# More zero matmuls in the opening, `v` of block 1 in quarters, and other engines for a few scalings and squares, in a fused attention and MLP kernel

## The chip, the core and the metric

The kernel runs on one core of a Trainium2 chip. Five engines work side by side, each with an instruction stream of its own: TensorE (PE in the profile, with its weight loads as PEld), VectorE (DVE), ScalarE (ACT), GpSimd (POOL) and SyncE (SP). Transfers between the chip's memory and the core's on-chip memory are issued from the queues of SP, ACT and POOL. The metric is the device time of one execution in microseconds (us), lower is better. An execution consists of the span of the core's instructions and about 1.8 us around it.

## The reference

Two stages: a linear attention with a decay per head, in blocks along the sequence, and an MLP with a snake-like activation on its output.

```python
q, k, v: (4, 8, 768, 64) float32     lam: (8,)      # batch, heads, sequence, head size
w_in: (512, 2048)   w_out: (2048, 512)   alpha: (2048,)

# attention, block after block; Dmask holds lam ** (i - j) for j <= i
intra = (qb @ kb.T) * Dmask
out   = intra @ vb + (qb * lam ** (pos + 1)) @ kv_state
kv_state = lam ** block * kv_state + (kb * rev_pow).T @ vb

# MLP on x = out as (3072 tokens, 512)
h = x @ w_in
s = sin(alpha * h)
g = h + s * s / (alpha + 1e-9)
return (g @ w_out).astype(float32)
```

## The kernel before, in words

**Units of work.** The attention is done in 24 steps: step `s` covers one pair of batches, one block of 128 tokens (the kernel takes blocks twice as long as the reference's) and one half of the heads. Two neighbouring steps share a block `d = s // 2` of `k`, `q` and `v`. The MLP is done in 6 chunks of 512 tokens; a chunk needs the attention output of four steps. For chunk `c`, phase A(c) computes `h` for 16 column groups `m` of 128, and phase B(c) multiplies the activations with `w_out` for four token tiles.

**One attention step.** `sec(t=...)` transposes `q` and `k` on TensorE (L482) into a PSUM bank, which is copied out as `qkT` (L667). `sec(s=...)` makes the scores (L494), which VectorE masks into `S_m` (L612). `sec(o=...)` multiplies the masked scores with the scaled `v` (L506), adds the state's part (L516) and forms the state's increment (L529). `put_x` (L625) multiplies the result with a decay table and writes `xT`, the MLP's input; `Zs` (L635, L648) and `Zacc` (L630, L646) keep the state. `prep_v(s)` (L461) scales `v` of a step with `Lv` and rounds it to bf16, on GpSimd or VectorE. For steps 0 to 7 the transposes are TensorE's; from step 8 they are DMA transposes issued from SP (L328).

**One MLP group.** `grp_A(c, m)` does four matmuls into a PSUM bank (L684), ScalarE's sine into `t` (L688), a square into `u` (L695 on ScalarE, L696 on VectorE or GpSimd) and VectorE's `gT = u * r + h` (L698), which reads the bank once more and frees it. `grp_B` accumulates an output tile (L721), ScalarE copies it to `osb` (L728), and SP stores it (L734).

**The opening.** Before the first chunk, the kernel builds masks and decay tables and runs steps 0 to 3. In this stretch TensorE has little to do, and `keep_pe(b, n)` (L422) puts `n` matmuls of 128x128 by 128x512 on zeros into bank `b` between the steps, as ordinary instructions in TensorE's order. `alpha_ops` transposes `alpha` on TensorE and copies it with ScalarE; `alpha_ops2` makes `r = 1 / (alpha + 1e-9)` (aeps on GpSimd, reciprocal on VectorE). The loads of this stretch are issued from POOL's queue: `k`, `q`, `v` of blocks 0 and 1 (L314) and `w_in` in four blocks of four column groups (`w1_block`, L446), then `w_out` in four blocks (L451) and blocks 2 and 3 of `k`, `q`, `v`. With `by_step=True` a `load` is split by step as well as by batch, so that each `prep_v` waits only for its own half of the heads.

**What sets the order.** `rec` hands every operation to a planner with a duration, what it reads and writes, and extra predecessors (`after`). The planner gives it a start time; TensorE and SP take operations in the order of recording, VectorE, ScalarE and GpSimd may take one into an earlier gap of the plan. The program of each engine is then the operations in the order of their planned starts, with semaphore waits where the data asks for them. The order is fixed by the plan; on the chip each engine runs its stream strictly in that order and stands still where a wait is not yet met. Where several engines may do an operation, `fastest` takes the one with the earliest planned end:

```python
def fastest(choices, reads, writes, after=()):
    ...
    return min(choices, key=end)
```

For chunk 1 the square's engine was fixed by `("ACT", "POOL", "DVE")[m % 3]`; for chunks 0, 2 and 3 `fastest` chooses among the three; for chunks 4 and 5 it is given by a table. Inside chunk 0 and 1 phases, `AHEAD_A1` says after which group of A(1) the scalings of steps 8 and 9 are recorded, and `LAST_B0` where the last pieces of B(0) stand between the groups of A(1). From step 8 on, `steady(i)` records the work of step `i` and, two or three steps ahead, the scaling of `v` through `ahead`.

Of the kernel before, what the change touches and what calls it, by code (L numbers as in the profile page):

```python
# [187 lines left out]
def bass_lightning_attn__then__act_snake_kernel(  # L188
# [33 lines left out]
    with es:  # L222
# [20 lines left out]
        Zacc = ring("Zacc", 2, [128, 2, 2 * D], F32)  # L243
# [87 lines left out]
        def clear_pads():  # L331
            for x in q2p:
                rec("DVE", lambda e, x=x: e.memset(x[:, 0:2 * H + 2:2 * H + 1, :], 0.0), 0.1, writes=["pad"])
# [83 lines left out]
        def keep_pe(b, n):  # L417
            z = maskf[:, :].bitcast(BF16)

            def pe(e):  # L420
                for _ in range(n):
                    last = e.matmul(PS[:, b, :], z[:, 0:128], z[:, :])  # L422
                return last
            rec("PE", pe, (0.427 if P.free["PE"] < 5 else 0.216) * n, reads=["maskf"], writes=bk(b))
# [7 lines left out]
                reads=["alpha_r", "identf"], writes=bk(b))  # L432
            rec("ACT", lambda e: e.copy(alpha_sb[:, :], PS[:, b, 0:NM]), 0.2, reads=bk(b), writes=["alpha"])

        def alpha_ops2():
            rec("POOL", lambda e: e.tensor_scalar_add(aeps_sb[:, :], alpha_sb[:, :], 1e-9), 0.2,
                reads=["alpha"], writes=["aeps"])
            rec("DVE", lambda e: e.reciprocal(r_sb[:, :], aeps_sb[:, :]), 0.2, reads=["aeps"], writes=["r"])

        def w_load(fn, keys, slot, n, after):  # L440
            return rec("POOL", fn, 0, writes=keys, slot=slot, nbytes=131072 * n, after=after)
# [29 lines left out]
        def sec(t=None, o=None, s=None, tb=None, sb_=S_BK, ob=O_BK, peek=False, t_engs=("DVE", "ACT"), via=False, x_first=False, z_late=None, later=False):  # L471
# [140 lines left out]
                    rec("DVE", lambda e: e.tensor_tensor(s_out, s_in, mask_b, ALU.mult), 1.25,  # L612
                        reads=keys_s + ["mask.0", "mask.1"], writes=[f"S_m.{s % RS}"])

            def put_O(part=None):
                z = PS[:, ob:ob + 2, 256:384]
                acc = Zacc[ho]
                zs = Zs[o % 3][:, :, :, :].rearrange("p u a d -> p u (a d)")

                def put_x():  # L620
                    x, col = (o // 4) % NX, 256 * (no % 2)
                    xo = xT[x][:, 2 * ho:2 * ho + 2, col:col + 256].rearrange("p a (u i) -> p u a i", u=2)
                    xi = PS[:, ob:ob + 2, 0:256].rearrange("p u (a i) -> p u a i", a=2)
                    X_b = bass.AP(Xt, (2 * ho * NB + no) * 128, [[HS * NB * 128, 128], [0, 2], [NB * 128, 2], [1, 128]])
                    rec("DVE", lambda e: e.tensor_tensor(xo, xi, X_b, ALU.mult), 0.72,  # L625
                        reads=keys_o + [f"X.{2 * ho + a}.{no}" for a in range(2)],
                        writes=[f"x.{x}.{o % 4}"])

                def first_state():
                    rec("ACT", lambda e: e.copy(acc[:, :, :], z), 0.4, reads=keys_o, writes=[f"Zacc.{ho}"])  # L630

                if part != 1 and no > 0:
                    put_x()
                if has_Z and no == 0:
                    rec("ACT", lambda e: e.copy(zs, z), 0.37, reads=keys_o, writes=[f"Zs.{o % 3}"])  # L635
                if no == 0:
                    put_x()
                if part == 0:
                    return
                if has_Z and no == 0:  # L640
                    if z_late is None:
                        first_state()
                    else:
                        z_late.append(first_state)
                elif has_Z:
                    rec("DVE", lambda e: e.tensor_tensor(acc[:, :, :], z, acc[:, :, :], ALU.add), 0.42,  # L646
                        reads=keys_o + [f"Zacc.{ho}"], writes=[f"Zacc.{ho}"])
                    rec("POOL", lambda e: e.tensor_copy(zs, acc[:, :, :]), 0.42,  # L648
                        reads=[f"Zacc.{ho}"], writes=[f"Zs.{o % 3}"])

# [108 lines left out]
        load(0, "k")  # L759
        load(0, "q")  # L760
        consts()
        keep_pe(0, 15)
        iotas()
        consts3()
        load(1, "k")
# [7 lines left out]
        mask_u([P.ops[-1]])  # L773
        sec(t=1, tb=(2, 3), t_engs=("ACT",))
        clear_pads()
        load(0, "v", eng="POOL", by_step=True)
        load(1, "v", eng="POOL")
        w1_block(0, 4)
        w1_block(4, 4)
        decay_table(2, NB, (2, 3))  # L780
        sec(s=0, sb_=4)
        sec(s=1, sb_=6)
        keep_pe(0, 4)
        sec(t=2, tb=(0, 1), t_engs=("ACT",))
        t2 = P.ops[-1]
        sec(t=3, tb=(2, 3), t_engs=("DVE",))
        prep_v(0, ("DVE",))
        sin_table([t2])
        prep_v(1, ("POOL",))
        zl = []  # L790
        keep_pe(4, 2)
        sec(s=2, sb_=0)
        sec(s=3, sb_=2)
        alpha_ops(6)
        prep_v(2, ("POOL",))
        prep_v(3, ("DVE",))
        alpha_ops2()
        w1_block(8, 4)
        w1_block(12, 4)
        sec(o=0, ob=4, z_late=zl)  # L800
        keep_pe(6, 2)
        sec(o=1, ob=6, z_late=zl)
        keep_pe(0, 5)
        o2 = sec(o=2, ob=0, later=True)
        o3 = sec(o=3, ob=2, later=True)
        for f in o2, o3:
            f(0)
        for f in zl:
            f()
        for f in o2, o3:  # L810
            f(1)

        npr = [10]

        def ahead(s):
            while npr[0] <= min(s, NSTEP - 1):
                prep_v(npr[0])
                npr[0] += 1

        def steady(i):  # L820
# [35 lines left out]
                else:  # L856
                    load(d, x, after=[op], us=(u,))

        AHEAD_A1 = {9: 8, 11: 9}
        LAST_B0 = {1: (2, 3), 3: (3, 3)}  # L860
        every, low = range(8), range(4)
        B0_SEC = {3: dict(t=4, tb=(6, 7)), 4: dict(t=5, s=4, tb=(6, 6)), 6: dict(t=6, s=5, tb=(7, 7)),
# [5 lines left out]
        for c in range(NCH):  # L868
            for m in range(NM):
                op = grp_A(c, m, every if m < 12 else (6, 7, 2, 3) if c == 1 else range(2, 4) if m == 15 and c else range(4, 8),  # L870
                      (SQ.get(m, "POOL"),) if c > 3 else (("ACT", "POOL", "DVE")[m % 3],) if c == 1 else ("POOL", "ACT", "DVE"))
                if c == 0:
                    loads(*ISSUE_A0.get(m, ()))
                feed("A", c, m, op)
                if c == 1 and m in AHEAD_A1:
                    prep_v(AHEAD_A1[m], ("POOL",))
                if c == 1 and m in LAST_B0:
                    grp_B(0, *LAST_B0[m], low)
                if c > 1 and m in (3, 7, 11):
                    grp_B(c - 1, 3, m // 4 + 1, low)  # L880
            b_seq = [(s4, m4) for m4 in range(4) for s4 in range(2)] + [(2, m4) for m4 in range(4)] + [(3, 0)]
            if c == 0:
                b_seq = [(s4, m4) for m4 in range(3) for s4 in range(4)] + [(0, 3), (1, 3)]
            if c == NCH - 1:
                b_seq.pop()
            for i, (s4, m4) in enumerate(b_seq):
                if c == 0:
                    loads(*ISSUE_B0.get(i, ()))
                op = grp_B(c, s4, m4, low)
                feed("B", c, i, op)  # L890
                if c == 0 and i in (6, 7, 8, 9):
                    prep_v(i - 2, ("DVE",) if i == 9 else ("POOL",))
                if c == 0 and i in B0_SEC:
                    sec(**B0_SEC[i])
                if c == 1 and i == 0:
                    sec(s=8)
                at = SEC1 if c == 1 else SEC
                if c > 0 and i in at and 4 * (c + 1) + at[i] < NSTEP:
                    steady(4 * (c + 1) + at[i])
# [35 lines left out]
```

## Time and profile before

| What | Value |
|---|---|
| time, median of 13 runs | 224.74 us (223.29 to 227.07) |
| profiled execution: time | 223.29 us |
| profiled execution: span of the core | 221.5 us |
| instructions | 5397 |
| TensorE busy | 201.9 us (91%) |
| VectorE busy | 148.3 us (67%) |
| ScalarE busy | 112.0 us (51%) |
| GpSimd busy | 100.0 us (45%) |
| mean granted TensorE clock | 0.992 |
| moved by DMA | 29.99 MB, mean 135 GB/s |
| `prep_v` on GpSimd / on VectorE | 16 / 8 instructions |

The profiled execution is the fastest of the 13: its time of 223.29 us is 1.79 us more than its span, and 1.45 us below the median. Times inside the profile count from the first instruction. The engines' busy times overlap, so their sum is no time; what counts at each place is which wait ends last there. A line of the timeline gives the start, the duration, the engine and line, what is written from what is read, the shapes, the count, and in square brackets how long the engine had been idle before it and what ended that idle time. Where a wait was for several semaphores, the one that came last is named.

### The profile page before, as it was taken

To read this page: it belongs to the slowest core of one execution; us is meant where nothing else is said; L and a number is where in the kernel's file an instruction comes from. 1 tells how busy PE (TensorE), PEld (TensorE's weight loads), DVE (VectorE), ACT (ScalarE), POOL (GpSimd) and SP (SyncE) were. 2 spreads that over 40 slices of the span, in tenths; PEclk is the share of its full clock that TensorE was granted. 3 is DMA by queue.
4 is the path that set the end of the run, shared out by engine and by line. 5 is a ranking of instruction groups with operands and counts; after the bars stand their busy time and mean duration, and the time that the engine had idled before them with its cause. 6 is when DMAs were issued, how large, how long until landed. Compare 5 with 4: busy or idle time off the path is not lost.

```text
span 221.5 us, 5397 instructions
## 1 busy us (share of the span) xinstructions
PE 201.9 (91%) x2282; PEld 100.4 (45%) x2317; DVE 148.3 (67%) x218; ACT 112.0 (51%) x185; POOL 100.0 (45%) x137
## 2 busy tenths in 40 slices
PE   7458899978999869999999999999999999999994
PEld 3234343444544335444455444455444544444453
DVE  2766699438358986679987688775678764477300
ACT  3952599220389702188923488602568321778030
POOL 7969890313653835247060431235564410555300
PEclk9996999999999999999999999999999999999999
DMA  6999999972899998999999998598900104102044
GB/s 63 145 212 184 202 190 218 206 115 24 97 198 220 243 200 142 224 224 193 220 161 216 175 128 180 109 112 201 155 23 22 29 0 108 37 0 50 0 95 95
DMA packets 69256, 29.99 MB, mean 135 GB/s; under 512 B 53216, under 2 KB 65776, under 8 KB 69232
## 3 DMA queue, kind: packets, MB, share of 16 engines
q0 software_dynamic: 30240, 12.59, 46.6%
q1 hardware_dynamic: 38736, 16.98, 37.3%
q8 instruction: 18, 0.29, 0.6%
q10 hardware_dynamic: 256, 0.08, 0.2%
q14 instruction: 6, 0.05, 0.1%
HBM read 27.28 MB, written 6.29 MB: 152 GB/s over the span
## 4 chain that ended last, share of the span: by engine, by line
PE 76%; DVE 8%; POOL 6%; DMA 4%; issue 3%; ACT 1%; POOLq 0%
PE PS L721 33%; PE PS L684 32%; DMA w<-in_moe_w_in_dram 4%; DVE gT L698 4%; PE PS L506 3%; PE PS L494 2%; PE PS L516 2%; POOL v L314 2%; DVE u L696 2%; DVE S_m L612 2%; PE PS L748 2%; POOL k L314 1%; PE PS L482 1%; POOL q L314 1%; PE PS L529 1%
## 5 line engine op out<-in xcount | busy, mean ns | idle before, releaser
L684 PE MATMUL PS<-xT,w 128*128 128x512 bf16 x376 | 85.7, 379 | 2.4 <-DMA w<-in_moe_w_in_dram 1.0
L721 PE MATMUL PS<-w,gT 128*128 128x512 bf16 x344 | 82.3, 379 | 3.4 <-issue 3.2
L698 DVE SCALAR_TENSOR_TENSOR gT<-u,r_sb,PS 128x512 bf16<-128x512 bf16 x96 | 69.4, 745 | 19.0 <-POOL u L696 13.2
L688 ACT ACTIVATE t<-PS,alpha_sb 128x512 bf16<-128x512 f32 x96 | 63.1, 680 | 23.0 <-PE PS L684 22.1
L684 PEld LDWEIGHTS PS<-xT,w 128*128 128x128 bf16 x384 | 36.8, 98 | 48.1 <-DVE gT L698 2.2
L721 PEld LDWEIGHTS PS<-w,gT 128*128 128x128 bf16 x368 | 34.0, 98 | 39.8
L728 ACT COPY osb<-PS 128x512 f32<-128x512 f32 x23 | 13.4, 584 | 57.1 <-PE PS L721 57.1
L612 DVE TENSOR_TENSOR S_m<-PS,mask 128x1024 bf16<-128x1024 f32 x24 | 29.2, 1222 | 17.2 <-PE PS L494 17.1
L696 POOL TENSOR_TENSOR u<-t 128x512 bf16<-128x512 bf16 x27 | 27.7, 1041 | 26.0 <-ACT t L688 25.8
L461 POOL TENSOR_TENSOR v<-v,Lv 128x512 bf16<-128x512 f32 x16 | 17.3, 1093 | 24.9 <-DMA v<-in_v_dram 24.9
L314 POOL DMA_DIRECT2D k<-in_k_dram x24 | 17.0, 714 | 22.5 <-PE PS L721 17.7
L625 DVE TENSOR_TENSOR xT<-PS,Xt 128x512 bf16<-128x512 f32 x24 | 16.3, 682 | 10.7 <-PE PS L516 10.6
L695 ACT ACTIVATE u<-t 128x512 bf16<-128x512 bf16 x36 | 22.7, 629 | 1.5
L696 DVE TENSOR_TENSOR u<-t 128x512 bf16<-128x512 bf16 x33 | 20.0, 605 | 2.6 <-ACT t L688 2.6
L314 POOL DMA_DIRECT2D q<-in_q_dram x24 | 16.5, 694 | 6.4 <-PE PS L721 4.0
L648 POOL CAST Zs<-Zacc 128x256 bf16<-128x256 f32 x16 | 7.1, 450 | 26.6 <-DVE Zacc L646 26.5
L506 PE MATMUL PS<-S_m,v 64*64 64x128 bf16 x384 | 10.2, 225 | 3.9 <-DVE S_m L612 1.8
L506 PEld LDWEIGHTS PS<-S_m,v 64*64 64x64 bf16 x384 | 6.4, 108 | 13.9 <-issue 9.1
L422 PE MATMUL PS<-maskf 128*128 128x512 bf16 x25 | 8.7, 497 | 1.6 <-DVE maskf L363 1.2
L667 ACT COPY qkT<-PS 128x1024 bf16<-128x1024 bf16 x5 | 5.1, 1012 | 10.1 <-PE PS L482 10.1
L461 DVE TENSOR_TENSOR v<-v,Lv 128x512 bf16<-128x512 f32 x8 | 6.7, 842 | 2.8 <-DMA v<-in_v_dram 2.8
L516 PE MATMUL PS<-qM,Zs 64*64 64x128 bf16 x112 | 8.1, 222 | 0.1
(53 smaller groups left out, 106.4 us busy)
## 6 DMA issues: line engine op xcount, KB each, us to landing
out_dram<-osb SPq DMA_DIRECT2D x46, 128.0 KB, 2.7
v<-in_v_dram SPq DMA_DIRECT2D x16, 256.0 KB, 5.2
k<-in_k_dram POOLq DMA_DIRECT2D x24, 128.0 KB, 4.8
q<-in_q_dram POOLq DMA_DIRECT2D x24, 128.0 KB, 5.0
w<-in_moe_w_in_dram POOLq DMA_DIRECT2D x4, 512.0 KB, 7.9
w<-in_moe_w_out_dram POOLq DMA_DIRECT2D x4, 512.0 KB, 12.7
v<-in_v_dram POOLq DMA_DIRECT2D x6, 256.0 KB, 11.8
v<-in_v_dram POOLq DMA_DIRECT2D x4, 128.0 KB, 4.3
```

The lines of the kernel that those rows point to most:

```text
L314: lambda e, u=u, a=a, h0=h0, h1=h1: e.dma_start(dst[r][half(u), h0:h1, :], a), 0,
L461: rec(eng, lambda e: e.tensor_tensor(v2[c][:, :, :], src, L_b, ALU.mult), dur, reads=reads, writes=writes)
L506: return e.matmul(dst, v2[o % RC][half(u), hid(h, tj), :], S_part(o, u, h, tj), start=start, stop=True, skip_group_check=True)
L612: rec("DVE", lambda e: e.tensor_tensor(s_out, s_in, mask_b, ALU.mult), 1.25, reads=keys_s + ["mask.0", "mask.1"], writes=[f"S_m.{s % RS}"])
L625: rec("DVE", lambda e: e.tensor_tensor(xo, xi, X_b, ALU.mult), 0.72, reads=keys_o + [f"X.{2 * ho + a}.{no}" for a in range(2)], writes=[f" ...
L684: last = e.matmul(PS[:, i, :], w1[:, kc, 128 * m:128 * (m + 1)], xT[x][:, kc, :], start=(kc == 0), stop=(kc == NKC - 1))
L688: rec("ACT", lambda e: e.activation(t16[tt][:, :], PS[:, i, :], ACTF.Sin, scale=alpha_sb[:, m:m + 1]), 0.7, reads=bk(i) + ["alpha"], write ...
L695: return e.activation(u16[tt][:, :], t16[tt][:, :], ACTF.Square)
L696: return e.tensor_tensor(u16[tt][:, :], t16[tt][:, :], t16[tt][:, :], ALU.mult)
L698: rec("DVE", lambda e: e.scalar_tensor_tensor(out=gT[g][:, m, :], in0=u16[tt][:, :], scalar=r_sb[:, m:m + 1], in1=PS[:, i, :], op0=ALU.mul ...
L721: last = e.matmul(PS[:, bank, :], gT[g][:, m, 128 * s4:128 * (s4 + 1)], w2[:, m, :], start=(m == 0), stop=(m == NM - 1))
L728: rec("ACT", lambda e: e.copy(osb[o][:, :], PS[:, bank, :]), 0.6, reads=bk(bank), writes=[f"o.{o}"])
```

## The change

The diff does the following:

- `keep_pe` gets one matmul more at the start (16 instead of 15), a new one after step 1's transposes, and 5, 4, 6, 4 and 2 instead of 4, 2, none, 2 and 5 between the steps that follow: 38 instead of 28.
- Block 1 of `v` is loaded in four quarters, as block 0 was already.
- The second block of `w_in` is recorded after the sine's table load and made to wait for it.
- `v` of step 0 is scaled on GpSimd instead of VectorE. From step 10 on every scaling is given to GpSimd; before, the planner chose.
- Step 0's output part is recorded before `prep_v(3)`. `alpha`'s transpose moves behind step 1, into bank 4, and the reciprocal and the first two `Zacc` additions are tied behind step 3's `put_x`.
- In A(1) the square's engine is the planner's choice instead of a fixed rotation, and for the last two groups it is ScalarE. The scalings of steps 8 and 9 are recorded after groups 13 and 15 instead of 9 and 11.

```diff
--- before.py
+++ after.py
@@ -432,10 +432,10 @@
                 reads=["alpha_r", "identf"], writes=bk(b))
             rec("ACT", lambda e: e.copy(alpha_sb[:, :], PS[:, b, 0:NM]), 0.2, reads=bk(b), writes=["alpha"])
 
-        def alpha_ops2():
+        def alpha_ops2(after):
             rec("POOL", lambda e: e.tensor_scalar_add(aeps_sb[:, :], alpha_sb[:, :], 1e-9), 0.2,
                 reads=["alpha"], writes=["aeps"])
-            rec("DVE", lambda e: e.reciprocal(r_sb[:, :], aeps_sb[:, :]), 0.2, reads=["aeps"], writes=["r"])
+            rec("DVE", lambda e: e.reciprocal(r_sb[:, :], aeps_sb[:, :]), 0.2, reads=["aeps"], writes=["r"], after=after)
 
         def w_load(fn, keys, slot, n, after):
             return rec("POOL", fn, 0, writes=keys, slot=slot, nbytes=131072 * n, after=after)
@@ -612,7 +612,7 @@
                     rec("DVE", lambda e: e.tensor_tensor(s_out, s_in, mask_b, ALU.mult), 1.25,
                         reads=keys_s + ["mask.0", "mask.1"], writes=[f"S_m.{s % RS}"])
 
-            def put_O(part=None):
+            def put_O(part=None, after=()):
                 z = PS[:, ob:ob + 2, 256:384]
                 acc = Zacc[ho]
                 zs = Zs[o % 3][:, :, :, :].rearrange("p u a d -> p u (a d)")
@@ -644,7 +644,7 @@
                         z_late.append(first_state)
                 elif has_Z:
                     rec("DVE", lambda e: e.tensor_tensor(acc[:, :, :], z, acc[:, :, :], ALU.add), 0.42,
-                        reads=keys_o + [f"Zacc.{ho}"], writes=[f"Zacc.{ho}"])
+                        reads=keys_o + [f"Zacc.{ho}"], writes=[f"Zacc.{ho}"], after=after)
                     rec("POOL", lambda e: e.tensor_copy(zs, acc[:, :, :]), 0.42,
                         reads=[f"Zacc.{ho}"], writes=[f"Zs.{o % 3}"])
 
@@ -759,7 +759,7 @@
         load(0, "k")
         load(0, "q")
         consts()
-        keep_pe(0, 15)
+        keep_pe(0, 16)
         iotas()
         consts3()
         load(1, "k")
@@ -773,48 +773,51 @@
         mask_u([P.ops[-1]])
         sec(t=1, tb=(2, 3), t_engs=("ACT",))
         clear_pads()
+        keep_pe(4, 1)
         load(0, "v", eng="POOL", by_step=True)
-        load(1, "v", eng="POOL")
+        load(1, "v", eng="POOL", by_step=True)
         w1_block(0, 4)
-        w1_block(4, 4)
         decay_table(2, NB, (2, 3))
         sec(s=0, sb_=4)
         sec(s=1, sb_=6)
-        keep_pe(0, 4)
+        keep_pe(0, 5)
         sec(t=2, tb=(0, 1), t_engs=("ACT",))
         t2 = P.ops[-1]
         sec(t=3, tb=(2, 3), t_engs=("DVE",))
-        prep_v(0, ("DVE",))
+        prep_v(0, ("POOL",))
         sin_table([t2])
+        w1_block(4, 4, after=[P.ops[-1]])
         prep_v(1, ("POOL",))
         zl = []
-        keep_pe(4, 2)
+        keep_pe(4, 4)
         sec(s=2, sb_=0)
         sec(s=3, sb_=2)
-        alpha_ops(6)
         prep_v(2, ("POOL",))
+        keep_pe(6, 6)
+        sec(o=0, ob=4, z_late=zl)
         prep_v(3, ("DVE",))
-        alpha_ops2()
         w1_block(8, 4)
         w1_block(12, 4)
-        sec(o=0, ob=4, z_late=zl)
-        keep_pe(6, 2)
+        keep_pe(6, 4)
         sec(o=1, ob=6, z_late=zl)
-        keep_pe(0, 5)
+        alpha_ops(4)
+        keep_pe(0, 2)
         o2 = sec(o=2, ob=0, later=True)
         o3 = sec(o=3, ob=2, later=True)
         for f in o2, o3:
             f(0)
+        x3 = [op for op in P.ops if op.eng == "DVE"][-1:]
         for f in zl:
             f()
         for f in o2, o3:
-            f(1)
+            f(1, x3)
+        alpha_ops2(x3)
 
         npr = [10]
 
         def ahead(s):
             while npr[0] <= min(s, NSTEP - 1):
-                prep_v(npr[0])
+                prep_v(npr[0], ("POOL",))
                 npr[0] += 1
 
         def steady(i):
@@ -856,7 +859,7 @@
                 else:
                     load(d, x, after=[op], us=(u,))
 
-        AHEAD_A1 = {9: 8, 11: 9}
+        AHEAD_A1 = {13: 8, 15: 9}
         LAST_B0 = {1: (2, 3), 3: (3, 3)}
         every, low = range(8), range(4)
         B0_SEC = {3: dict(t=4, tb=(6, 7)), 4: dict(t=5, s=4, tb=(6, 6)), 6: dict(t=6, s=5, tb=(7, 7)),
@@ -868,7 +871,7 @@
         for c in range(NCH):
             for m in range(NM):
                 op = grp_A(c, m, every if m < 12 else (6, 7, 2, 3) if c == 1 else range(2, 4) if m == 15 and c else range(4, 8),
-                      (SQ.get(m, "POOL"),) if c > 3 else (("ACT", "POOL", "DVE")[m % 3],) if c == 1 else ("POOL", "ACT", "DVE"))
+                      (SQ.get(m, "POOL"),) if c > 3 else ("ACT",) if c == 1 and m > 13 else ("POOL", "ACT", "DVE"))
                 if c == 0:
                     loads(*ISSUE_A0.get(m, ()))
                 feed("A", c, m, op)
```

## The prediction

> **What bounds the kernel now.** I read the busy rows by slice first, then the chain that ended last, then the timelines around the two stretches in which TensorE stands still.
>
> ```profile
> PE   7458899978999869999999999999999999999994
> PEclk9996999999999999999999999999999999999999
> PE 76%; DVE 8%; POOL 6%; DMA 4%; issue 3%; ACT 1%; POOLq 0%
> ```
>
> A slice is 5.54 us, counted here from 0. From slice 17 (94 us) on TensorE is full, so nothing in the change can gain there. It is thin in slices 0 to 3, in slice 8 (a gap of 0.78 us at 47.7 for which the profile shows no wait, and which the change does not touch) and in slices 13 and 14 (72 to 83 us), the end of A(1). Only in slice 3 is the granted clock low.
>
> The opening ends when the first MLP group starts:
>
> ```profile
> 14.83 0.69 DVE L461 TENSOR_TENSOR v<-v,Lv 128x512 bf16<-128x512 f32 x1 [1.28 <-DMA v<-in_v_dram]
> 15.44 2.35 DVE L612 TENSOR_TENSOR S_m<-PS,mask 128x1024 bf16<-128x1024 f32 x2
> 18.53 1.30 POOL L461 TENSOR_TENSOR v<-v,Lv 128x512 bf16<-128x512 f32 x1
> 21.51 1.52 DVE L625 TENSOR_TENSOR xT<-PS,Xt 128x512 bf16<-128x512 f32 x2 [1.28 <-PE PS L516]
> 23.10 10.06 PEld L684 LDWEIGHTS PS<-xT,w 128*128 128x128 bf16 x48 [0.97 <-issue]
> 18.00:20.00 2.00, 2.00 (x5) 0.45 (x3) 1.76 (x4) 0.64 (x2) 1.98 (x3) 0.50 1.21 197
> ```
>
> The chain names a `w_in` transfer, landed at 22.79, as what released the first group, but that is the second block. The first group needs the first block, issued at 12.61 and landed 7.6 us later, at 20.2. What came last is step 3's `xT`: 21.51 + 1.52 = 23.03, and weights load at 23.10. Behind it stand VectorE, which waits in order for `v` and so masks steps 2 and 3 only from 15.44, though their scores were ready at 14.3; GpSimd, which scales step 2 until 19.83; and five zero matmuls and step 2 at half clock (17.75 to 21.17 in windows of half a microsecond).
>
> The end of A(1):
>
> ```profile
> 73.80 1.90 PE L684 MATMUL PS<-xT,w 128*128 128x512 bf16 x8 [0.69 <-DVE gT L698]
> 76.03 2.34 DVE L696 TENSOR_TENSOR u<-t 128x512 bf16<-128x512 bf16 x1
> 78.41 1.41 DVE L698 SCALAR_TENSOR_TENSOR gT<-u,r_sb,PS 128x512 bf16<-128x512 bf16 x2
> 79.73 1.22 DVE L612 TENSOR_TENSOR S_m<-PS,mask 128x1024 bf16<-128x1024 f32 x1
> 76.03 2.05 POOL L461 TENSOR_TENSOR v<-v,Lv 128x512 bf16<-128x512 f32 x2
> 81.09 0.42 PE L506 MATMUL PS<-S_m,v 64*64 64x128 bf16 x16 [1.49 <-DVE S_m L612]
> ```
>
> A square that takes 0.42 us elsewhere on VectorE takes 2.34 while GpSimd scales steps 8 and 9 (2.05). Behind it wait two `gT`, step 8's mask, and TensorE: 0.7 us for a bank at 73.80 and 1.49 for the mask.
>
> **The opening, part by part.** *POOL's queue.* `v` goes from six issues to eight: 8.78 + 8 x 0.647 = 13.95, so `w_in`'s first block is issued 1.3 us later. It landed 2.0 us after the last `v` (18.2), so I put it at 20.5; should the issue set it, 13.95 + 7.6 = 21.55. Step 0's scaling waits for its `v` (landed 14.83) and takes GpSimd's 1.04: done at 15.92 instead of VectorE's 15.5. The second block's issue (0.83) waits for the sine table, whose small activation ended at 15.08, so this new wait is over before the scaling is, and what queues behind it on POOL (two scalings, two `w_in` blocks, `w_out`) loses only the 0.83: 16.75. Before, this issue went out at 13.4, while GpSimd had nothing else to do. Then steps 1 and 2 at 1.04 each: 17.79 and 18.83. The upper quarter pair of block 1 has landed by then: pieces took 5.4 to 6.3 us from issue, so 11.9 + 5.5 = 17.4 for step 2, and 13.2 + 5.5 to 6.3 = 18.7 to 19.5 for step 3. Later `w_in` blocks: 18.83 and 19.66 instead of 17.68 and 19.79; they landed with 4.8 and 5.9 us to spare (25.5 for a group at 30.3; 27.9 for 33.8), the second block with 4. A start 1.4 us earlier, and the second issue's 15.92 + 9.4 = 25.3 in the worst case, stays at what its group wants (25.1). Later loads had 4.8 us or more.
>
> *VectorE.* Without step 0's `v`, the two masks run from 14.05 to 16.45 (before 17.79), step 0's `xT` to 17.25, step 3's `v` (waits for its quarter) to about 19.4, step 1's `xT` to 20.0. The reciprocal (0.25) lies behind step 3's `xT`, and the first `gT` comes 2 us after TensorE's start, so it costs nothing; late, each 0.1 us would move A(0).
>
> *TensorE.* The added zero matmuls lie in waits: one before the identity (free from 6.0 to 8.0), one while `qkT` is copied (8.8 to 9.3), one before the load of `q` at 12.04, two before step 2's scores. The six run from 14.3 to 15.65, before `v` at 15.92; the four behind step 0 from 16.5 to 17.4, before step 1's `v` at 17.79; the last two to 18.95. `alpha`'s transpose, now in step 0's bank, waits for its `xT` (17.25), which is past. So 10 more matmuls at 0.216 (2.16 us) cost about 0.1: step 2 starts at 18.95, not 18.83. At half clock the twelve would cost 12 x 0.21 = 2.5, and about 1.7 would show.
>
> *The end.* Steps 2 and 3 take 0.83 from start to start and 1.05 to their end (step 3 before, at full clock: 21.25 to 22.30): step 3 ends at 20.85, its `xT` 0.7 later, weights load at 21.65. Gain 23.10 - 21.65 = 1.45. If step 3's `v` lands at 19.5, it is 1.0. I take 1.4. A(0) then runs at its own pace, set by ScalarE and VectorE (4.9 and 4.85 of 5 us), and B(0) had no wait for a transfer, so the gain is carried on.
>
> **The clock: row and rule.** The row shows 0.50 from 17.75 for 3.4 us, though TensorE's longest gap in the 3.4 us before was 1.15 us and it was busy for some 1.45 (43%); the 3.4 us before that had 2.3 (66%) and kept the clock. The Trainium skill, "TensorE: Matmul & The Clock Gate", Part 1 (HAM oscillation), lets the clock fall for gaps above about 3.4 us. By that rule nothing would have fallen, and the added matmuls buy nothing; by the row, the same stretch will be busy for 2.75 of 3.4 us (80%) and stays at full clock. That is worth step 2's 1.43 against 1.05, 0.4 us of the 1.4. I take the row. Zeros count as work for it: the fifteen matmuls at the start went from 0.43 to 0.22 us apart within 4 us.
>
> **A(1).** The choice by earliest planned end gives VectorE and ScalarE in turn: the planner has ScalarE free when its sine ends (0.65 to go, against GpSimd's 1.05), and A(2), which has this rule, shows them in turn. So the five GpSimd squares go, and ScalarE gets 9 instead of 6. A(0), the same pattern, took ScalarE 24.19 to 39.18 = 15.0 for 16 sines and 8 squares. Walking through ScalarE's lines with two output copies between gives its last square at 76.8 to 77.5 (before 77.09). VectorE has no square in the last two groups, and `gT` and masks beside a GpSimd scaling keep their 0.72 and 1.23. So the last `gT` ends at 78.3 instead of 79.82, the mask at 79.45 instead of 80.95, and step 8 starts at 79.5 instead of 81.09. TensorE itself, with bank waits of 0.3, is ready at 79.0. Steps 8 and 9 are scaled from 74.9 (landing) on, in time. Gain 1.5 to 2.1; I take 1.7. DMA transposes for step 12 landed at 88.7 for a use at 91.6: cover enough. For ScalarE's three more squares the cover is TensorE's 18 groups at 0.865; without it they cost 3 x 0.53 = 1.6.
>
> **Scaling on GpSimd from step 10.** Five instructions move (9 of 14 were there): 5 x 0.68 off VectorE, 5 x 1.04 onto GpSimd, used 2 to 3 steps later in a stage where TensorE is the bound. Row: beside GpSimd's scalings, VectorE's square took 2.03 at 102.29 and a scaling 1.93 at 114.69, and TensorE lost 0.2 or less. The Trainium skill, "SBUF — State Buffer", section Who interferes with whom, speaks against this edit: an instruction of VectorE with both inputs on chip is blocked for the whole of a GpSimd one that reads there. By the rule alone, five moved scalings may add 5 x 1.04 = 5.2 us of stalls; by the row they stay off TensorE. Bounds: 0.3 gained (a wait at 87.85) to 5.2 lost; I take 0, by the row.
>
> **Sum.** Against the profiled 223.29 us (span 221.5 and 1.79 around it, the fastest of 13): -1.4 - 1.7 = -3.1, so 220.2 for such an execution. I carry the difference to the median: 224.74 - 3.1 = 221.6, and 0.1 of it for executions whose clock fell elsewhere: 221.5.
>
> **The rivals.**
> 1. *Only A(1) gains.* The last quarter of `v` or a late `w_in` block takes the place of `xT`, or the clock falls all the same. For: landings of 5.4 to 6.3 us and two more issues. Against: 2 us before the block is due. -1.7, so 223.0; with half of A(1) gone, no change.
> 2. *Only the opening gains.* ScalarE's three squares (1.6 us) put its last square at 78.7, and step 8 starts at 80.8: -1.4 - 0.3 = -1.7, 223.0. For: ScalarE 97% busy in A(0). Against: TensorE's two extra groups (1.73). Here the choice could also turn out otherwise than the plan suggests, with squares on GpSimd behind two scalings; then A(1) is as before.
> 3. *Slower: GpSimd's scalings hold VectorE in the MLP stage.* Each moved one blocks a square, `gT` is late, banks run out, TensorE waits. Five at up to 1.24 (1.93 - 0.69) are 6.2: 223.29 - 3.1 + 6.2 on the profiled run, +3.1, 227.8 on the median. It decides from 0.85 us each reaching TensorE (4.2 in all). For: stalls of 1.2 to 1.6 are there already. Against: they cost 0.2.
> 4. *The zero matmuls don't hold the clock*, and their 2.5 us at half speed go before step 2: A(0) starts 1.7 later than before instead of earlier, the sum is 0, 224.7.
>
> **How the numbers follow.** The measurement can tell about 0.5%: below 223.6 is faster, above 225.9 slower. Both gains (220.3 to 222.6): 0.62. Rivals 1 and 2: 0.20, of which 0.17 below 223.6. Rival 4: 0.08 (no change), rival 3: 0.06 (slower), mixtures 0.04 (0.03 of it slower). Faster 0.62 + 0.17 + 0.01 = 0.80, same 0.03 + 0.08 = 0.11, slower 0.09. The range takes in both gains at their upper ends with a clock gain in other executions (219.9) and most of rivals 1 and 2 (223.8).
>
> **What would show it.** Right: granted clock 1.0 from 6 to 30 us; masks of steps 2 and 3 from 14; weights of A(0) loading near 21.7; no square of VectorE over 1.2 us at the end of A(1); step 8 of TensorE 3 us earlier than 81.09. Wrong: A(0) released by a transfer, clock at 0.5 across 15 to 21 us, L684 or L721 waiting for `gT` beyond 94 us.

## The result and the profile after

The changed kernel takes 221.54 us, median of 11 executions (219.84 to 226.02), against 224.52 for the kernel before (48 executions in all comparisons). The ratio is 0.9866, 95% interval 0.9837 to 0.9895: 1.3% faster. The forecast was 221.5. A ratio leaves out executions more than 1.5% above the fastest of their kernel; medians here are over all executions. The profiled execution is the median one: 221.54 us, span 219.7, where before's was 223.29 and 221.5.

The busy rows by slice of the changed kernel (a slice is now 5.49 us):

```profile
PE   7787999989999998699999999999999999999994
...
PEclk9999999999999999999999999999999999999999
```

The granted clock no longer drops in slice 3. The thin pair of slices 13 and 14 is gone, but a new thin slice stands at 16 (88 us), where TensorE was nearly full before.

The opening, from the timelines of VectorE and TensorE and the table of stretches (a stretch of time, for example 18 to 20 us; columns there: length, busy time of PE, PEld, DVE, ACT, POOL, granted clock, DMA share, GB/s):

```profile
13.61 2.36 DVE L612 TENSOR_TENSOR S_m<-PS,mask 128x1024 bf16<-128x1024 f32 x2 [0.61 <-PE PS L494]
...
17.74 1.21 DVE L461 TENSOR_TENSOR v<-v,Lv 128x512 bf16<-128x512 f32 x1 [0.36 <-DMA v<-in_v_dram]
...
18.87 2.32 DVE L625 TENSOR_TENSOR xT<-PS,Xt 128x512 bf16<-128x512 f32 x3
...
21.55 2.75 PE L684 MATMUL PS<-xT,w 128*128 128x512 bf16 x12 [1.10 <-DVE xT L625]
...
18.00:20.00 2.00, 1.93 (x79) 1.36 (x79) 1.87 (x3) 1.10 (x4) 1.93 (x4) 1.00 1.17 178
```

The masks of steps 2 and 3 start at 13.61 instead of 15.44, the last `xT` ends at 21.19 instead of 23.03, and the clock from 18 to 20 us is 1.00 instead of 0.50. `xT` is still what comes last; the first matmul of A(0) moves from 23.35 to 21.55, a gain of 1.8 us.

The end of A(1) and B(1):

```profile
74.31 0.63 ACT L695 ACTIVATE u<-t 128x512 bf16<-128x512 bf16 x1
...
75.63 1.22 DVE L612 TENSOR_TENSOR S_m<-PS,mask 128x1024 bf16<-128x1024 f32 x1
...
73.68 2.05 POOL L461 TENSOR_TENSOR v<-v,Lv 128x512 bf16<-128x512 f32 x2
75.67 0.72 POOL L314 DMA_DIRECT2D q<-in_q_dram  x1
...
76.91 0.42 PE L506 MATMUL PS<-S_m,v 64*64 64x128 bf16 x16 [0.32 <-DVE S_m L612]
...
89.48 0.42 PE L506 MATMUL PS<-S_m,v 64*64 64x128 bf16 x16 [2.14 <-DMA qM<-q]
...
81.34 3.13 SPq L328 DMA_TRANSPOSE qM<-q  x2
```

The last square is now ScalarE's (0.63 us), where VectorE's took 2.34. Step 8 starts at 76.91 instead of 81.09, 4.18 us earlier. That includes 1.8 from the opening and 0.66 in B(0), where the gap of 0.78 us at 47.7 is absent; A(1) itself gives the remaining 1.72. But 2.14 us of it are given back at 89.48, before step 11: TensorE waits for the DMA transposes of `q` of block 6. The last load of that `q` went out at 75.67, behind the scalings of steps 8 and 9, and landed at 81.3; the transposes went out at 81.34 and 83.0 and landed 2.9 and 6.5 us later, the second at 89.5. In the kernel before, GpSimd's and SP's rows were:

```profile
78.02 1.40 POOL L314 DMA_DIRECT2D q<-in_q_dram  x2
...
83.54 3.16 SPq L328 DMA_TRANSPOSE qM<-q  x2
```

There both loads of `q` stood behind the same two scalings, and the last went out at 78.7, 3.0 us later than now. It landed at 83.5, the transposes took 3.4 us each, and the second landed at 88.7. So in the changed kernel the load goes out 3.0 us earlier and lands 2.2 us earlier, but the last transpose lands 0.8 us later. A(2) starts at 91.24 instead of 93.05: of 4.18 us, 1.81 are left, and the span is shorter by just that, 1.8.

### The profile page after: what moved, and what is told of

Read it like the earlier page. It is cut to its first block, busy times and chain, and to the rows that moved or that the text cites. A ratio compares the mean times of both kernels' runs of the same rounds, so it can differ in the third digit from the quotient of the medians.

```text
span 219.7 us, 5418 instructions
## 1 busy us (share of the span) xinstructions
PE 204.0 (93%) x2292; PEld 101.0 (46%) x2327; DVE 144.2 (66%) x214; ACT 113.9 (52%) x188; POOL 100.6 (46%) x140
## 4 chain that ended last, share of the span: by engine, by line
PE 74%; POOL 7%; DVE 6%; ACT 5%; issue 4%; DMA 3%; POOLq 0%; DVEq 0%; ACTq 0%
PE PS L721 32%; PE PS L684 30%; PE PS L506 4%; ACT t L688 3%; DVE gT L698 3%; DMA qM<-q 3%; PE PS L494 2%; PE PS L516 2%; POOL v L314 2%; DVE S_m L612 2%; PE PS L748 2%; ACT u L695 1%; PE PS L529 1%; POOL k L314 1%; PE PS L482 1%
## 5 line engine op out<-in xcount | busy, mean ns | idle before, releaser
L688 ACT ACTIVATE t<-PS,alpha_sb 128x512 bf16<-128x512 f32 x96 | 63.0, 681 | 22.4 <-PE PS L684 21.8
L684 PEld LDWEIGHTS PS<-xT,w 128*128 128x128 bf16 x384 | 36.8, 98 | 47.7 <-DVE gT L698 2.6
L461 POOL TENSOR_TENSOR v<-v,Lv 128x512 bf16<-128x512 f32 x22 | 22.8, 1054 | 29.8 <-DMA v<-in_v_dram 29.7
L696 POOL TENSOR_TENSOR u<-t 128x512 bf16<-128x512 bf16 x22 | 22.5, 1041 | 20.1 <-ACT t L688 20.1
L695 ACT ACTIVATE u<-t 128x512 bf16<-128x512 bf16 x39 | 24.6, 630 | 1.7
L696 DVE TENSOR_TENSOR u<-t 128x512 bf16<-128x512 bf16 x35 | 18.7, 534 | 5.2 <-ACT t L688 5.2
L422 PE MATMUL PS<-maskf 128*128 128x512 bf16 x35 | 11.2, 471 | 1.5 <-DVE maskf L363 1.2
L314 POOL DMA_DIRECT2D v<-in_v_dram x12 | 7.9, 699 | 0.0
```

The costliest lines, as they stand in the source:

```text
L314: lambda e, u=u, a=a, h0=h0, h1=h1: e.dma_start(dst[r][half(u), h0:h1, :], a), 0,
L461: rec(eng, lambda e: e.tensor_tensor(v2[c][:, :, :], src, L_b, ALU.mult), dur, reads=reads, writes=writes)
L684: last = e.matmul(PS[:, i, :], w1[:, kc, 128 * m:128 * (m + 1)], xT[x][:, kc, :], start=(kc == 0), stop=(kc == NKC - 1))
L688: rec("ACT", lambda e: e.activation(t16[tt][:, :], PS[:, i, :], ACTF.Sin, scale=alpha_sb[:, m:m + 1]), 0.7, reads=bk(i) + ["alpha"], write ...
L695: return e.activation(u16[tt][:, :], t16[tt][:, :], ACTF.Square)
L696: return e.tensor_tensor(u16[tt][:, :], t16[tt][:, :], t16[tt][:, :], ALU.mult)
```

## The experiments

In all of them the times are medians of all executions and the ratio is to the kernel before on the same chip (223.75, 224.38 and 224.93 us on three chips). Three questions were open. Is the opening's gain the clock or the order? What is A(1) worth, and who takes it back? What does the scaling on GpSimd cost? I use the mean granted clock of each execution throughout: a fall to one half for 3.4 us, as in before's profile, lowers it by 1.7/221.5, to 0.992. The diffs are shortened, without their context. Each experiment has one kept profile, of one execution.

### The added zero matmuls taken away

```diff
-        keep_pe(0, 16)
+        keep_pe(0, 15)
-        keep_pe(4, 1)
-        keep_pe(0, 5)
+        keep_pe(0, 4)
-        keep_pe(4, 4)
+        keep_pe(4, 2)
-        keep_pe(6, 6)
-        keep_pe(6, 4)
+        keep_pe(6, 2)
```

> The changed kernel without the thirteen zero matmuls that it adds or enlarges (15, none, 4, 2, none, 2 and 2 instead of 16, 1, 5, 4, 6, 4 and 2). Theory (the gain is the new order of VectorE and GpSimd; the clock is a small term): the granted clock falls in the opening in some executions, A(0)'s weights load at 21.3 to 21.8 us, the time is 221.5 to 222.3, at most 0.5 us above the changed kernel. Rival (the zero matmuls carry the gain through the clock): A(0) starts at 22.5 or later and the time is 223 to 224.5.

225.04 us (12 executions), ratio 1.0008 [0.9961, 1.0056]. The whole gain of the change is gone. The mean clock is below 0.995 in all 12 executions (0.970 to 0.992). Stretches of its profile, and its first MLP matmul:

```profile
14.00:16.00 2.00, 0.10 (x8) 0.10 (x12) 2.00 (x2) 0.80 (x2) 1.68 (x3) 1.00 0.66 157
...
18.00:20.00 2.00, 2.00 (x51) 1.07 (x43) 1.82 (x2) 0.87 (x4) 2.00 (x3) 0.50 1.11 144
```
```profile
24.07 6.17 PE L684 MATMUL PS<-xT,w 128*128 128x512 bf16 x20 [1.02 <-DMA w<-in_moe_w_in_dram]
```

For contrast, the same stretch of the changed kernel:

```profile
14.00:16.00 2.00, 1.53 (x36) 0.68 (x36) 1.97 (x2) 0.53 (x2) 2.00 (x3) 1.00 0.65 142
```

The new order leaves TensorE busy for 0.10 us between 14 and 16, where the changed kernel has zero matmuls (1.53). The clock then falls for 3.4 us from 18.0, step 3's `xT` ends at 23.79, A(0) starts at 24.07, later than in the kernel before, and the clock falls once more at 24.8.

### The zero matmuls alone

On the kernel before, with its order kept; the six stand ahead of step 0's outputs.

```diff
+        keep_pe(4, 1)          # after clear_pads()
+        keep_pe(7, 6)          # before sec(o=0)
-        keep_pe(0, 15); keep_pe(0, 4); keep_pe(4, 2); keep_pe(6, 2); keep_pe(0, 5)
+        keep_pe(0, 16); keep_pe(0, 5); keep_pe(4, 4); keep_pe(6, 4); keep_pe(0, 2)
```

> The kernel before with the change's zero matmuls alone (16, 1, 5, 4, 6, 4 and 2, the six into bank 7 ahead of step 0's output), in the order of before. Clock theory, as it stands after the first four runs: the granted clock is 1.0 in nearly all executions, and the time is that of the executions of before with an undisturbed clock, 222.0 to 222.6; the remaining 1.5 us to the changed kernel are the new order. Rival (the matmuls only stand in the way of the old order): 224 or more.

222.04 us (6), ratio 0.9888 [0.9836, 0.9940]: as far as the measurement can tell, the whole of the change's 0.9866. Four of six executions keep the clock at 1.0 (220.0 to 224.29 us); two are at 0.992. The profile is of one of these two, in which the fall comes later than in the kernel before, at A(0)'s start:

```profile
22.00:24.00 2.00, 1.94 (x5) 0.76 (x5) 0.26 (x1) 0.42 (x1) 2.00 (x4) 0.50 1.23 204
```
```profile
13.40 0.69 DVE L461 TENSOR_TENSOR v<-v,Lv 128x512 bf16<-128x512 f32 x1
```

The second line is VectorE's scaling of step 0, still in the old order. It starts at 13.40 without a wait, where the profile of the kernel before has it at 14.83 after 1.28 us: the landing of `v` differs between these two executions. In this one the old order loses nothing to step 0's `v`, and A(0) starts at 22.06 although step 0 stays on VectorE.

### The six alone, and five left ahead of step 2

The changed kernel with, of the added zero matmuls, only the six (the first diff without the line on `keep_pe(6, 6)`):

> The changed kernel with only the six zero matmuls before step 0's output added; the other additions are left out as in the kernel with 25 of them. Theory (the clock is lost in the stretch from 14 to 16 us, where TensorE was busy for 0.10 of 2 us with 25 matmuls): the six fill it, the clock is 1.0 in most executions, and the time is within 0.5 us of the changed kernel, 220.5 to 221.5. Rival (all thirteen are needed): the clock falls in most executions, 222.5 to 225.

222.21 us (6), ratio 0.9848 [0.9795, 0.9902]; the clock is kept in 3 of 6 executions, where without the six it was kept in none of 12. With all thirteen it is kept in 10 of 17 (both measurements of the changed kernel together). So the six carry much of it; that they carry less than all thirteen, six executions cannot tell.

Then the zero matmuls alone again, with `keep_pe(0, 5)` before step 2 left at five:

> The kernel before with the added zero matmuls, but with five in front of step 2 as before instead of two (41 in all), to tell the clock from the shorter row in front of step 2. If the clock is what counts: as with two, 220.5 to 222.3, clock 1.0 in most executions. If the shorter row counts (3 x 0.216 = 0.65 us less in TensorE's order ahead of steps 2 and 3): 0.6 us above that or more, 222.5 and up.

223.42 us (12), ratio 0.9939 [0.9904, 0.9975]. The clock is at 0.997 or above in 10 of 12, and A(0) starts at 22.01, as with two of them (22.06): the longer row costs nothing there. A(2) starts at 91.06, 2.0 us earlier than in the kernel before, but then a wait comes up in it. VectorE and TensorE:

```profile
94.79 0.69 DVE L461 TENSOR_TENSOR v<-v,Lv 128x512 bf16<-128x512 f32 x1 [2.67 <-DMA v<-in_v_dram]
...
99.80 2.54 DVE L696 TENSOR_TENSOR u<-t 128x512 bf16<-128x512 bf16 x1
...
107.39 1.90 PE L684 MATMUL PS<-xT,w 128*128 128x512 bf16 x8 [1.48 <-DVE gT L698]
```

VectorE runs the same operations in the same order as in the kernel before. It stands 2.67 us for a `v` that landed hardly earlier than there (the same scaling starts at 95.18 in the kernel before, after a wait of 1.07). With no time in hand it then spends 2.54 us on a square beside two scalings on GpSimd (2.03 in the kernel before), and TensorE waits for a bank. So this run, too, supports that more zero matmuls hold the clock, and its time shows how an earlier start is lost to a transfer that did not come forward with it. That is read from one of its twelve executions.

### The opening alone, and A(1) alone

The changed kernel with both A(1) edits undone and scalings from step 10 left to the planner:

```diff
-        ("ACT",) if c == 1 and m > 13 else ("POOL", "ACT", "DVE")
+        (("ACT", "POOL", "DVE")[m % 3],) if c == 1 else ("POOL", "ACT", "DVE")
-        AHEAD_A1 = {13: 8, 15: 9}
+        AHEAD_A1 = {9: 8, 11: 9}
-        prep_v(npr[0], ("POOL",))
+        prep_v(npr[0])
```

> The changed opening alone: A(1)'s squares, the recording of the scalings of steps 8 and 9 and the scalings from step 10 on are as before. Theory (two separate stalls removed): A(0) starts at 21.2 as in the changed kernel, step 8 of TensorE starts about 1.7 us later than there (78.6), and no wait for q's DMA transposes follows, so the time is 222 to 223. Rival (the whole gain is the opening's, A(1)'s is given back to the transposes): the time is that of the changed kernel, 221.5 or less.

220.83 us (6), ratio 0.9877 [0.9836, 0.9918]: not to be told from the changed kernel. The clock is 1.0 in all six. In its profile (its slowest execution, 223.81) the old waits at A(1)'s end are there, 0.69 us for a bank at 72.85 and the one for step 8's mask, and the one for `qM`:

```profile
80.03 0.42 PE L506 MATMUL PS<-S_m,v 64*64 64x128 bf16 x16 [1.38 <-DVE S_m L612]
...
91.79 0.42 PE L506 MATMUL PS<-S_m,v 64*64 64x128 bf16 x16 [1.41 <-DMA qM<-q]
```

So the transposes of `q` are late here too: the wait comes with the earlier opening, not with A(1)'s edits alone.

The reverse, the first two edits of that diff made on the kernel before:

> The kernel before with the change's A(1) alone: the planner's choice of the squares' engines, ScalarE for the last two, the scalings of steps 8 and 9 recorded later. Theory: no square of VectorE over 1.2 us at the end of A(1), step 8 of TensorE starts at 79.4 instead of 81.09; up to 2 us of it may go to a wait for q's transposes before step 11, so the time is 222.8 to 224.3. Rival (all of it is lost in that wait): no difference, 224.5.

227.06 us (6), ratio 1.0104 [1.0036, 1.0171]: slower, which neither expectation had. TensorE and VectorE around the end of A(1):

```profile
79.59 0.42 PE L506 MATMUL PS<-S_m,v 64*64 64x128 bf16 x16 [0.32 <-DVE S_m L612]
...
86.56 0.42 PE L506 MATMUL PS<-S_m,v 64*64 64x128 bf16 x16 [3.26 <-issue]
...
84.83 0.69 DVE L461 TENSOR_TENSOR v<-v,Lv 128x512 bf16<-128x512 f32 x1 [3.10 <-DMA v<-in_v_dram]
85.44 0.68 DVE L625 TENSOR_TENSOR xT<-PS,Xt 128x512 bf16<-128x512 f32 x1
```
```profile
88.00:90.00 2.00, 2.00 (x6) 0.63 (x5) 1.63 (x3) 0.59 (x1) 0.28 (x1) 0.50 0.93 192
```

Step 8 starts at 79.59 instead of 81.09: the squares bring 1.5 us. Then step 9 waits 3.26. The profile names no operand ("issue"); VectorE's rows show why. The planner gave it the scaling of step 10, which waits 3.10 us in order for `v` of block 5, and step 8's `xT` stands behind it until 85.44; the `Zacc` addition after that ends at 86.45, and step 9 starts 0.1 us later. After that wait the clock is 0.50 from 88 to 90. All six executions have a mean clock of 0.977 to 0.990; in the profile it also fell once at A(0)'s start (22.7).

### The scaling from step 10 left to the planner

The changed kernel with only the last line of that diff undone:

> The changed kernel with the scalings from step 10 on left to the planner, as before. By the prediction they stay off TensorE's path: the same time as the changed kernel within 0.4 us. Rival 1 of the prediction's third case (they hold VectorE): 1 us or more faster than it. Rival 2 (step 10's scaling waits for its load on GpSimd and holds the state's copy behind it, 1.6 us seen in the kernel with q's loads moved): 0.3 to 1 us faster.

221.77 us (6), ratio 0.9867 [0.9826, 0.9907]. By ratio nothing changes; the four executions that keep the clock take 221.13 to 221.77, against 219.74 to 221.60 (median 220.4) for the ten of the changed kernel. The profile is of the slowest (225.18 us):

```profile
83.78 0.69 DVE L461 TENSOR_TENSOR v<-v,Lv 128x512 bf16<-128x512 f32 x1 [4.70 <-DMA v<-in_v_dram]
```
```profile
85.50 0.64 PE L506 MATMUL PS<-S_m,v 64*64 64x128 bf16 x16 [4.83 <-issue]
```

It is the wait of the run before, longer. The clock is 1.0 through the opening here and falls at 85.3, behind this wait. In the changed kernel GpSimd waits for the same load (4.24 us, until 80.64), but of step 8 only the copy `Zs` stands behind it (81.63), which step 10 needs and not step 9.

### The late `q`, two ways

In the kernel `kq(d)` stands for the loads of `k` and `q` of block `d`, `vt(d)` for those of `v`, and `tu(d)` for the DMA transposes; `FEED` says after which group each goes out. First the four loads of `k` and `q` of block 6, each after one of groups 11 to 14 of A(1), ahead of the scalings on POOL:

```diff
-                ("A", 1): dict(enumerate(kq(5)[1:] + tu(4) + vt(4) + tu(5) + vt(5) + kq(6)[:3])),
-                ("B", 1): dict(enumerate(kq(6)[3:] + [None] + tu(6) + vt(6) + kq(7) + vt(7))),
+                ("A", 1): dict(enumerate(kq(5)[1:] + tu(4) + vt(4) + tu(5) + vt(5))),
+                ("B", 1): dict(enumerate([None] * 2 + tu(6) + vt(6) + kq(7) + vt(7))),
...
+                if c == 1 and 10 < m < 15:
+                    d, x, u = kq(6)[m - 11]
+                    load(d, x, after=[op], us=(u,))
```

> The changed kernel with the four loads of k and q of block 6 issued after groups 11 to 14 of A(1) instead of 13 to 15 and the first group of B(1), so that none of them stands behind the scalings of steps 8 and 9 on GpSimd. Theory (the 2.1 us wait of step 11 comes from q's last load, which the scalings hold up): the transposes of q start at 78 to 80 instead of 81.3 and 83.0, the wait is gone, the time is 219.5 to 220.5. Rival (the wait comes from the transposes' own landing, 6.5 us against 2.9, or moves to another transfer): the wait stays in part, the time is 221 to 221.8.

220.70 us (6), ratio 0.9886 [0.9849, 0.9923]. The wait for `qM` is gone, and another stands in its place; GpSimd and TensorE:

```profile
83.70 1.04 POOL L461 TENSOR_TENSOR v<-v,Lv 128x512 bf16<-128x512 f32 x1 [8.34 <-DMA v<-in_v_dram]
85.23 0.42 PE L506 MATMUL PS<-S_m,v 64*64 64x128 bf16 x16 [1.61 <-POOL Zs L648]
```

GpSimd waits 8.34 us for `v` of block 5, and the copy `Zs`, which TensorE needs, is queued behind. The wait moved by one transfer.

Then all operands of blocks 4 to 6 earlier: the loads of B(0) from group 4 on, the transposes and `v` in A(1) ahead of block 6.

```diff
-        FEED = {("B", 0): dict(enumerate(kq(4) + kq(5)[:1], 9)),
-                ("A", 1): dict(enumerate(kq(5)[1:] + tu(4) + vt(4) + tu(5) + vt(5) + kq(6)[:3])),
-                ("B", 1): dict(enumerate(kq(6)[3:] + [None] + tu(6) + vt(6) + kq(7) + vt(7))),
+        FEED = {("B", 0): dict(enumerate(kq(4) + kq(5) + vt(4), 4)),
+                ("A", 1): dict(enumerate(tu(4) + tu(5) + vt(5) + kq(6))),
+                ("B", 1): dict(enumerate([None] * 2 + tu(6) + vt(6) + kq(7) + vt(7))),
```

> The changed kernel with the loads and DMA transposes of blocks 4 to 6 moved ahead: the loads of block 4 and of k and q of block 5 start after group 4 of B(0) instead of 9 (where the DMA engines had nothing to do), and what follows moves up by five to seven places. Theory (A(1)'s gain of 1.7 us is real and is given back only because the operands of steps 10 to 12 land late): the waits of 1.6 to 2.1 us in B(1) are gone, TensorE reaches A(2) at 89.3 instead of 91.2, and the time is 218.5 to 219.8. Rival (the gain is lost elsewhere too, or the earlier loads collide with those of blocks 2 and 3): 220.5 or more.

219.83 us (4, 219.80 to 220.55), ratio 0.9822 [0.9780, 0.9865]. TensorE:

```profile
77.45 0.42 PE L506 MATMUL PS<-S_m,v 64*64 64x128 bf16 x16 [0.41 <-DVE S_m L612]
...
89.57 3.61 PE L684 MATMUL PS<-xT,w 128*128 128x512 bf16 x16
```

No wait of B(1) is over 0.41 us, and A(2) starts at 89.57, 1.67 us earlier than in the changed kernel's profile. With the A(1) edits undone on top of that:

> The same earlier loads and transposes, with A(1)'s squares and the recording of the scalings of steps 8 and 9 as before the change. Theory: step 8 starts 1.5 us later for want of its mask, with no later wait that hides it, so the time is 1.2 to 1.8 us above the kernel with the early loads alone, 220 to 221.3. Rival (A(1)'s edits are worth nothing even when the operands come early, because the scalings of steps 8 and 9 then lie elsewhere): the same time within 0.4 us.

220.20 us (5), ratio 0.9827 [0.9785, 0.9869]:

```profile
90.25 3.62 PE L684 MATMUL PS<-xT,w 128*128 128x512 bf16 x16
```

With the operands in time, the A(1) edits are worth 0.7 us by the profiles (90.25 - 89.57) and 0.4 by the medians, which the intervals cannot tell from nothing; the expectation had 1.2 to 1.8. The bank wait of 0.69 is back (at 72.42), but step 8 no longer waits for its mask.

### Both versions once more

> The changed kernel itself once more, beside the others of this group on the same chip: 220.5 to 221.6, ratio 0.985 to 0.99.

> The changed kernel with the loads of blocks 4 to 6 moved ahead, once more, beside the changed kernel on the same chip. Theory (its gain over the changed kernel is the waits for late operands in B(1)): 0.7 to 1.5 us below the changed kernel, and closer runs. Rival (the difference lay between chips): within 0.4 us of it.

The changed kernel: 222.75 us (6, 219.74 to 226.61), ratio 0.9809 [0.9748, 0.9869]. With early operands: 220.47 us (6, 219.98 to 223.27), ratio 0.9823 [0.9774, 0.9872]. The ratios do not separate the two. What seems to separate them is how often an execution keeps its clock: over all runs 10 of 17 against 9 of 10, with medians of 221.54 and 220.2; these are few executions. In this second profile of the changed kernel the wait before step 11 is 0.67 us; the second transpose of `q` took 5.2 us and landed at 87.9:

```profile
88.01 0.42 PE L506 MATMUL PS<-S_m,v 64*64 64x128 bf16 x16 [0.67 <-issue]
...
89.70 3.62 PE L684 MATMUL PS<-xT,w 128*128 128x512 bf16 x16
```

A(2) starts at 89.70 there and the span is 218.2, 3.3 us shorter than before's profile: the same kernel loses 2.14 us or 0.67 by how a transpose happens to land.

## Why the prediction was right, and where it was not

*The total* came out (221.5 forecast, 221.54 measured), but in part by luck: two errors cancelled. The opening was put at 1.4 us; the opening alone has a ratio of 0.9877, which is about 2.8 us of the 223.75 on that chip. A(1) was put at 1.7; on top of the opening it adds nothing that can be measured (0.9866 against 0.9877), and made alone it costs 1.0%.

*The opening's order* came out as worked out: masks from 13.61 (14.05 said), step 0's scaling done at 15.60 (15.92), its `xT` at 17.37 (17.25), A(0)'s first matmul 1.8 us earlier where 1.4 was said, released by `xT` and not by `w_in`'s first block. But that the old order stood waiting for `v` was read from one execution; in another it did not wait. The gap in B(0) that the working left as it was (0.78 us at 47.7) is absent, but that is not the change's doing: it is absent with the zero matmuls alone and with A(1) alone as well, and a like gap stands elsewhere in other profiles (1.38 us at 51.9 with the opening alone). Its cause is open.

*The clock* is the term that was mis-sized. I put it at 0.4 us of the opening's 1.4, as step 2's matmuls at full speed, with the ten more zero matmuls at a cost of 0.1, and at another 0.1 for executions whose clock fell elsewhere. Without the added ones the change gains nothing (1.0008), and with them alone the old order has 0.9888. The working priced a fall of the clock at the place where before's profile showed it. It did not ask how often it falls (before: in 38 of 45 executions the mean clock is at or below 0.995, median 224.58; in the other seven it is 222.31). The difference of 2.27 between those groups is not the clock's price alone, since waits and falls come together. Nor did it ask whether the new order without zero matmuls would be thinner, which it is, with 0.10 of 2 us busy. The stretch that it put at 80% busy was so for 73% (2.48 of 3.4 us from 14.35), and kept the clock.

That the row was taken over the rule (Trainium skill, "TensorE: Matmul & The Clock Gate", Part 1, HAM oscillation) was right: by that rule the zero matmuls buy nothing, and their removal cost the whole gain. Another section of the same page, A second HAM failure mode, tells of a clock that goes back and forth where the matmul engine stands still briefly and often; the runs here side with that one, and it should have been weighed too.

Rival 4 fell in the profiled execution, where the clock is 1.0 throughout; in 7 of 17 executions the clock still falls somewhere. That these falls lie in the opening is unlikely. Four kernels with the same opening (the opening alone, the loads of `q` moved, and early operands with and without A(1)'s edits) kept the clock in 26 of 27 executions, and the one kept profile with this opening and a fall, that of the scaling left to the planner, has it behind a late operand. For the changed kernel itself no profile of such an execution exists, so this is not shown.

*A(1)*: mechanism and size were right up to step 8, 1.72 us against 1.7, and the choice of engines came out (ScalarE has 39 squares instead of 36, GpSimd 22 instead of 27). What failed is the step "DMA transposes for step 12 landed at 88.7 for a use at 91.6: cover enough". That cover of 2.9 us was less than the forecast's own sum of 3.1, and 4.18 us came together by step 8; and it took for granted that the landing stays at 88.7, where it came at 89.5 in one profile of the changed kernel and at 87.9 in the other. The place of the load behind the two scalings does not explain it, since it was the same before; moving the loads earlier did take the wait away, and uncovered the next late operand. So rival 2 (only the opening gains) was right in what it said of A(1), by outcome: the opening alone has 0.9877, the change 0.9866. Its number (223.0) was wrong, as the opening gained more, and its mechanism too, since ScalarE was in time.

*Scaling on GpSimd from step 10*, put at 0, cost nothing by the ratio (0.9866 with it, 0.9867 without), but it was not priced for what it prevents. Where the planner may choose VectorE, VectorE stood 3.10 and 4.70 us behind a load, and TensorE 3.26 and 4.83, each in one profile. That this is why A(1)'s edits made the kernel before 1.0% slower is argued from that profile; in the changed kernel the same freedom left the ratio as it was. Rival 3 fell: in the changed kernel's profile TensorE has no wait over 0.16 us from A(2) to the end, and the estimate of 5.2 us by the rule of the Trainium skill, "SBUF — State Buffer" (Who interferes with whom), did not come. Its mechanism can reach TensorE, though: with five zero matmuls left ahead of step 2, a square of 2.54 us beside two scalings, which were on GpSimd before the change too, was among what held VectorE ahead of a wait of 1.48.

*Still open*: how the 1.9 us between the two kernels' executions that kept the clock (222.3 and 220.4) divide between order, zero matmuls and A(1). The zero matmuls alone reach 220.0 to 224.29 in such executions. For the opening the profiles narrow it: A(0) starts at 22.01 and 22.06 with the zero matmuls alone, and between 21.3 and 21.8 in the nine profiles of the new order with all thirteen or the six of them, so the order is worth 0.2 to 0.7 us there. Why `v` and the transposes land at different times in different executions was not tried.

## What to carry to other kernels

Cheap filler for an engine whose clock is granted by use belongs in the thin stretches ahead of its work, judged by how busy it is over a few microseconds and not by its longest gap alone, and a reordering that makes a stretch thinner must be counted with it. Before a stall ahead of a stage is taken away, list the landing times of the next stage's transfers against the sum of all gains up to there; if the slack is smaller, move those loads with it. An operation that waits for a load does not belong on an in-order engine ahead of work that the bound engine needs, even where that engine does it faster.

## What was not expected of the hardware

- The clock falls for thin use, without a long gap: to 0.50 for 3.4 us after 3.4 us that were 42% busy with no gap over 1.15 us (before, 14.35 to 17.75), and after 3.4 us that were 61% busy with no gap over 0.61 us (zero matmuls alone, 18.0 to 21.4). The busy share does not settle it alone: 3.4 us at 55% kept the clock (A(1) alone, 15.95 to 19.35). Waits of 3.26 and 4.83 us in mid-kernel were followed by a clock of 0.50 as well.
- Zero matmuls hold it: with 13 of them more, 10 of 17 executions kept a mean clock above 0.995, without them none of 12.
- The same transfers differ between executions of the same or nearly the same program: `v` of step 0 was ready before 13.40 or at 14.83, and of two DMA transposes issued 1.7 us apart the second landed after 6.5 us in one execution of the changed kernel and after 5.2 in another, where the kernel before had 3.4.
